# Loads of x and of the rearranged Wo: 32 partitions at a time, or all 128

## The chip, the cores and the metric

The kernel runs on one core of a Trainium2 chip. The time is that of the device, in microseconds, from one launch; the median of three runs is given, with the lowest and the highest. A profile of one further execution tells what each engine did: PE multiplies matrices (PEld loads its weights), DVE, ACT and POOL work elementwise, SP issues most of the transfers. Transfers (DMAs) run beside the engines, on 16 DMA engines that all queues share.

## The reference

One block of a transformer on x (2048 rows of 640, bf16): layer norm, then two branches that read the normed rows and are added to x.

```python
xn = _layernorm(x, axis=-1)
return x + _A_ref(xn, A_wqkv, A_wo) + _B_ref(xn, B_w_gate, B_w_up, B_w_down)

# A: 32 heads of 20, each row sees itself and the 255 rows before it (W = 256)
qkv = (x @ wqkv).reshape(B, S, 3, H, Dh)
scores = einsum("bhqd,bhkd->bhqk", q, k) * Dh ** -0.5
p = softmax(where(mask, scores, -1e9))
out = einsum("bhqk,bhkd->bhqd", p, v).reshape(B, S, D) @ wo      # wo: 640 x 640

# B: a gated MLP, F = 1536
h = sigmoid(x @ w_gate) * (x @ w_up)
out = h @ w_down
```

## The kernel before, in words

The 2048 rows are worked in four chunks of 512 rows (CW). A tile has 128 partitions (P); a chunk of x is a tile xc of 128 partitions by 4 blocks (SBC) of 640 columns, 1280 bytes a block. There is one such buffer (pool xp), so a chunk's load waits until the chunk before it is used up.

**x.** Chunk 0 is loaded 128 rows at a time (load_rows, L135). Chunks 1 to 3 are loaded by load_x (L113 to L118) in another order of rows: the chunk's row 128a + 32n + t lies in partition 32a + t, block n. This order lets the later transposition of 32 by 32 blocks (turn_block, L244) and a pass through memory (turn_rows, L249 and L251) give the normed rows transposed, as xnT, which every product with weights reads. load_x makes one transfer for each a: it fills the partitions 32a to 32a + 31, all four blocks. load_x(1) stands at L700, load_x(2) within qk1 (behind its first block of k, L723), load_x(3) after the norms of chunk 2 (L724).

**Normalization.** ln_block (L208, L214 on DVE) takes mean and variance of one block of columns of xc, rstd_blocks (L222, L223 on POOL) the factor of all four, norm_block (L227) applies them.

**q and k.** proj_block (L266) makes 128 columns of q or k transposed in PSUM. DVE (q) or ACT (k) copies them to a tile st (L270, L272; six buffers), which frees the PSUM bank, and SP stores st to a scratch in memory (sq, sk, L274). spread (L287) loads the scratch back in the layout of the scores, as qT and kT. The scratch holds 32 rows for each head of 20; POOL clears the other 12 once (clear, L156). So that these clears do not compete with x, POOL first copies two numbers of chunk 1 of x to a tile, landed (L703), which waits for that chunk to land.

**Scores and values.** PE makes scores ps (L500), ACT their exponentials pT (L506), POOL and DVE mask them (select at L489, masks at L517), PE multiplies by v (acc, L533), DVE divides and transposes (L544 to L567) to oc.

**MLP and output.** g_gu: products pg and pu (L414, L423), tanh on ACT (L417), h on DVE (L427). g_out: y gathers h times w_down (L437) and oc times wo (L444); DVE adds x's rows (L448), which SP loads (L454) ahead of time and stores as output (L459).

**wo.** The rows of Wo must be in the order of oc. POOL copies Wo in memory to wo_i (turn_wo, L179), eight transfers handed out one by one in qk1, each behind a projection block. wo_i is laid out by group i (4), then 160 rows. load_wo (L182 to L185) later fills the tile wo with four transfers, each 32 partitions by 5 blocks of 640.

**Order of work.** All is written in one order. PE's work is mixed by a planner (class Fill): attention steps come in their order, and between them parts of the rest (fill.add, L726 to L745) are drawn by estimated cost. PSUM tiles of all but the scores come from one ring of four banks (ps_d): a product waits until the bank four tiles back has been read. Each engine and each queue works in order. SP's transfers go round eight semaphores, and a transfer waits until the one eight before it has landed.

The functions that the change touches:

Of the kernel before, what the change touches and what calls it, by code (L numbers as in the profile page):

```python
# [9 lines left out]
P = 128  # L10
S = 2048
D = 640
H = 32
DH = 20
F = 1536
DC = D // P
FC = F // P
CW = 512
NCH = S // CW
SBC = CW // P  # L20
HG = 4
NG = H // HG
# [13 lines left out]
BF16 = mybir.dt.bfloat16  # L36
# [33 lines left out]
def kernel(  # L70
# [11 lines left out]
    nc = tc.nc  # L82
    x2 = A_x.flatten_outer_dims()
# [27 lines left out]
    xc = {}  # L111

    def load_x(c):  # L113
        t = xp.tile([P, SBC, D], BF16, name="xc")
        xc[c] = t
        rows = x2[c * CW:(c + 1) * CW, :].rearrange("(a n t) d -> a t n d", a=SBC, n=SBC)
        for a in range(SBC):
            nc.sync.dma_start(out=t[32 * a:32 * a + 32], in_=rows[a])  # L118

    wqkv = const.tile([P, DC, 3 * D], BF16, name="wqkv")  # L120
    wqkv_r = A_wqkv.rearrange("(c p) n -> p c n", p=P)
# [3 lines left out]
    wo = const.tile([P, DC, D], BF16, name="wo")  # L125
# [28 lines left out]
    def clear(w):  # L154
        rows = scratch[w].rearrange("(h j) s -> h (j s)", j=32)[:, DH * CW:]
        nc.gpsimd.dma_start(out=rows.rearrange("h (a e) -> h a e", a=4), in_=zero[:, 0:3, :])  # L156
# [14 lines left out]
        for lo, hi in ((0, 3), (3, 6), (6, 8), (8, 10), (10, FC)):  # L171
            nc.sync.dma_start(out=wd[:, lo:hi, :], in_=wd_r[:, lo:hi, :])

    wo_i = tc.dram_tile([HG, NG * DH, D], BF16, name="wo_i")

    def turn_wo(r, side):
        to = wo_i.rearrange("i (r a d) n -> r a i (d n)", a=2, d=DH)
        rows = A_wo.rearrange("(a r i d) n -> r a i (d n)", a=2, i=HG, d=DH)
        nc.gpsimd.dma_start(out=to[r, side].rearrange("i (e w) -> e i w", e=16),  # L179
                            in_=rows[r, side].rearrange("i (e w) -> e i w", e=16))  # L180

    def load_wo():  # L182
        for i in range(HG):
            nc.sync.dma_start(out=wo[32 * i:32 * i + 32, :, :],
                              in_=wo_i[i].rearrange("(m j) n -> j m n", j=32))  # L185


    ident = const.tile([P, P], BF16, name="ident")
# [263 lines left out]
    def new_rows(c, s, name="rows", bufs=3, queue=nc.sync):  # L452
        rows = lnp.tile([P, D], BF16, name=name, bufs=bufs)
        queue.dma_start(out=rows, in_=xr[:, c * SBC + s, :])  # L454
        return rows
# [242 lines left out]
    banks.close()  # L698
    ps_s = banks.enter_context(tc.tile_pool(name="ps_s", bufs=1, space=bass.MemoryType.PSUM))
    load_x(1)  # L700
    load_gu(wg, B_w_gate, 0, FS // 2)
    landed = const.tile([P, 2], BF16, name="landed")
    nc.gpsimd.tensor_copy(out=landed, in_=xc[1][:, 0, 0:2])  # L703
    clear("q")
    clear("k")
    for k, _ in enumerate(g_qk(0)):
# [11 lines left out]
    def later(load, *args):  # L718
        load(*args)
        yield 0  # L720

    behind1 = {("qk"[n // 4], 1 + n % 4): (lambda n=n: turn_wo(n // 2, n % 2)) for n in range(2 * NP)}
    behind1["k", 0] = lambda: load_x(2)  # L723
    norms2 = itertools.chain(g_norms(2, True), later(load_x, 3))  # L724
    norms3 = g_norms(3, False)
    fill.add("gu0a", mix(g_gu(0, 0, 6), g_first(rstds1), 0), 6 * GU)  # L726
# [3 lines left out]
    fill.add("v1", mix(g_v(1), norms2, 2, 1, False), 40 * 136)  # L730
    fill.add("rest1", later(spread_rest, 1), 0)
    fill.add("wo", later(load_wo), 0)
    fill.add("gu0c", mix(g_gu(0, 9, 12), norms2, 0, 1, False), 3 * GU)
    fill.add("gu1a", mix(g_gu(1, 0, 2), norms2, 0, 1, False), 2 * GU)
# [46 lines left out]
    c = NCH - 1  # L781
# [5 lines left out]
    rows = [new_rows(c, s, queue=nc.scalar) for s in range(SBC - 1)]  # L787
# [58 lines left out]
```

## Time and profile before

| | |
|---|---|
| median of 3 runs | 308.87 us (308.83 to 309.37) |
| the profiled execution | 309.65 us, its span 308.0 us |
| PE busy | 302.9 us |
| ACT / DVE / POOL busy | 193.2 / 184.4 / 83.8 us |
| granted clock of PE | 1.00 |
| moved by DMA | 36.86 MB, 120 GB/s over the span |

Times in the profile are counted from the first instruction. A line of the timeline gives the start, the length, the engine, the source line, the operation, what it writes and reads, how often, and in brackets how long the engine stood before it and what ended that wait. SPq is SP's queue of issues: its lines tell when a transfer was issued, not when it landed. A row of the stages gives the busy times of the engines in a stretch, the granted clock, the mean busy share of the 16 DMA engines (it can pass 1, since packets overlap) and what they moved.

### The profile page before, as it was taken

Reading aid. Unit: us, or ns where it says so; the run is one execution under the profiler, and the core shown is the slowest. Engines: PE = TensorE matmul, PEld = TensorE weight load, DVE = VectorE, ACT = ScalarE, POOL = GpSimd, SP = SyncE. Lnnn points to the kernel's source line nnn. Section 1 sums busy time; section 2 is a strip of 40 time slices with the busy share of each in tenths; the row PEclk is TensorE's granted clock in tenths of the full one; section 3 lists DMA queues with packets and bytes.
Section 4 is the critical chain, followed back from the end, with each engine's and each line's share of the span. In section 5 each row is a group of like instructions: output and inputs, shape, how many; then the busy total and the mean of one; then the engine's idle time right before and its main releaser. Section 6 shows DMA issues by size and latency. Waiting matters only on the chain.

```text
span 308.0 us, 10147 instructions
## 1 busy us (share of the span) xinstructions
PE 302.9 (98%) x4431; PEld 168.2 (55%) x4431; DVE 184.4 (60%) x378; ACT 193.2 (63%) x183; POOL 83.8 (27%) x189
## 2 busy tenths in 40 slices
PE   7999999999999999999999999999999999999996
PEld 3654445564456655654456655644546765444774
DVE  5787449298984579577642666454383627465523
ACT  6923785977766458867655557777766466778000
POOL 5011234635314133422213122241314132221100
PEclk9999999999999999999999999999999999999999
DMA  7997739889927222721152113550000210000301
GB/s 213 347 306 238 266 102 309 220 248 320 198 94 199 85 72 93 228 80 47 43 128 72 39 65 99 163 192 2 3 2 2 70 41 23 2 2 2 88 21 64
DMA packets 35756, 36.86 MB, mean 120 GB/s; under 512 B 2944, under 2 KB 35456, under 8 KB 35712
## 3 DMA queue, kind: packets, MB, share of 16 engines
q1 hardware_dynamic: 34304, 33.84, 36.6%
q0 software_dynamic: 544, 1.61, 1.7%
q10 hardware_dynamic: 864, 0.77, 0.9%
q8 instruction: 34, 0.56, 0.8%
q14 instruction: 10, 0.08, 0.1%
HBM read 25.59 MB, written 11.44 MB: 120 GB/s over the span
## 4 chain that ended last, share of the span: by engine, by line
PE 97%; DMA 1%; ACT 1%; DVE 0%; issue 0%; SPq 0%
PE pg L414 18%; PE y L437 18%; PE pu L423 17%; PE pqk L266 15%; PE ps L500 9%; PE y L444 7%; PE acc L533 6%; PE pv L324 6%; PE pv L304 1%; DMA xc<-in_A_x_dram 1%; PE pvh L304 0%; PE pt L233 0%; ACT turn L640 0%; ACT turn L645 0%; DVE turn L651 0%
## 5 line engine op out<-in xcount | busy, mean ns | idle before, releaser
L506 ACT ACTIVATE pT<-ps 128x2048 bf16<-128x2048 f32 x75 | 140.8, 1877 | 56.0 <-PE ps L500 33.4
L489 POOL TENSOR_SCALAR_AFFINE_SELECT pT<-pT 64x256 bf16<-64x256 bf16 (+1 forms) x126 | 67.5, 536 | 181.0 <-ACT pT L506 122.9
L414 PE MATMUL pg<-xnT,wg 128*128 128x512 bf16 x240 | 59.9, 380 | 0.0
L423 PE MATMUL pu<-xnT,wu 128*128 128x512 bf16 x240 | 59.8, 380 | 0.0
L427 DVE SCALAR_TENSOR_TENSOR h<-th,pu 128x512 bf16<-128x512 f32 x48 | 32.9, 685 | 42.8 <-ACT th L417 25.7
L437 PE MATMUL y<-wd,h 128*128 128x320 bf16 (+2 forms) x396 | 56.8, 295 | 0.0
L266 PE MATMUL pqk<-xnT,wqkv 128*128 128x512 bf16 x200 | 45.8, 381 | 0.0
L437 PEld LDWEIGHTS <-h 128*128 128x128 bf16 x396 | 36.8, 98 | 15.9 <-issue 2.3
L517 DVE TENSOR_TENSOR pT<-pT,keep 128x512 bf16<-128x512 bf16 (+2 forms) x81 | 35.4, 444 | 15.6 <-ACT pT L506 14.7
L417 ACT ACTIVATE th<-pg 128x512 f32<-128x512 f32 x48 | 28.6, 595 | 20.2 <-PE pg L414 19.9
L423 PEld LDWEIGHTS <-wu 128*128 128x128 bf16 x240 | 22.3, 98 | 27.3 <-issue 2.2
L414 PEld LDWEIGHTS <-wg 128*128 128x128 bf16 x240 | 21.7, 98 | 26.4 <-issue 2.9
L266 PEld LDWEIGHTS <-wqkv 128*128 128x128 bf16 x200 | 22.6, 119 | 19.0 <-issue 1.5
L500 PE MATMUL ps<-qT,kT 20*64 20x320 bf16 (+4 forms) x1440 | 32.0, 260 | 0.0
L544 DVE STREAM_TRANSPOSE t<-acc 128x512 f32<-128x512 f32 x32 | 21.0, 694 | 17.9 <-PE acc L533 17.9
L448 DVE SCALAR_TENSOR_TENSOR rows<-y,rows 128x320 bf16<-128x320 f32 x30 | 14.4, 489 | 24.2 <-PE y L444 24.2
L500 PEld LDWEIGHTS <-kT 20*64 20x64 bf16 x1440 | 13.5, 103 | 27.2 <-issue 26.7
L444 PE MATMUL y<-wo,oc 128*128 128x320 bf16 (+2 forms) x165 | 24.2, 295 | 0.0
L533 PE MATMUL acc<-pT,v 64*32 64x320 bf16 (+4 forms) x1440 | 20.3, 253 | 0.5 <-issue 0.5
L533 PEld LDWEIGHTS <-v 64*32 64x32 bf16 x1440 | 17.0, 92 | 4.2 <-issue 1.6
L444 PEld LDWEIGHTS <-oc 128*128 128x128 bf16 x165 | 15.5, 98 | 6.7 <-issue 1.0
L324 PE MATMUL pv<-wqkv,xnT 128*64 128x320 bf16 x240 | 17.4, 300 | 0.0
(61 smaller groups left out, 173.3 us busy)
## 6 DMA issues: line engine op xcount, KB each, us to landing
qT<-sq SPq DMA_DIRECT2D x16, 256.0 KB, 4.2
kT<-sk SPq DMA_DIRECT2D x16, 256.0 KB, 4.3
xc<-in_A_x_dram SPq DMA_DIRECT2D x16, 160.0 KB, 4.0
sq<-st SPq DMA_DIRECT2D x20, 128.0 KB, 3.6
sk<-st SPq DMA_DIRECT2D x20, 128.0 KB, 2.9
out_dram<-rows SPq DMA_DIRECT2D x15, 160.0 KB, 1.8
wg<-in_B_w_gate_dram SPq DMA_DIRECT2D x4, 480.0 KB, 7.2
wu<-in_B_w_up_dram SPq DMA_DIRECT2D x4, 480.0 KB, 7.4
```

The costliest lines, as they stand in the source:

```text
L266: nc.tensor.matmul(ps, lhsT=wt[:, m, :], rhs=xnT[c][:, :, d, :], start=(d == 0), stop=(d == DC - 1))
L324: nc.tensor.matmul(ps[hf * U:(hf + 1) * U, 0:HALF], lhsT=xnT[c][:, s, d, rows], rhs=wqkv[:, d, 2 * D + hf * HALF:2 * D + (hf + 1) * HALF], ...
L414: nc.tensor.matmul(pg, lhsT=part(wg, d, f), rhs=xnT[c][:, :, d, :], start=(d == 0), stop=(d == DC - 1))
L423: nc.tensor.matmul(pu, lhsT=part(wu, d, f), rhs=xnT[c][:, :, d, :], start=(d == 0), stop=(d == DC - 1))
L427: nc.vector.scalar_tensor_tensor(out=h, in0=th, scalar=1.0, in1=pu, op0=ADD, op1=MULT)
L437: nc.tensor.matmul(y[:, 0:cut[1] - cut[0]], lhsT=ht[c, f][:, s * P:(s + 1) * P], rhs=wd[:, f, cut[0]:cut[1]], start=(f == 0), stop=False)
L444: nc.tensor.matmul(y[:, 0:cut[1] - cut[0]], lhsT=oc[c, m][:, s * P:(s + 1) * P], rhs=wo[:, m, cut[0]:cut[1]], start=False, stop=(m == DC - 1))
L489: nc.gpsimd.affine_select(out=part, in_=part, pattern=pattern, compare_op=GE, fill=0.0, base=-1 if sign > 0 else 0, channel_multiplier=sign)
L500: nc.tensor.matmul(ps[side * U:(side + 1) * U, i, col * U:(col + n) * U], lhsT=qk["k", kc, half][32 * i:32 * i + DH, 2 * r + side, kb * U: ...
L506: nc.scalar.activation(out=pt[:, :, 0:used, :], in_=ps[:, :, 0:used * U], func=EXP, scale=SCALE)
L517: nc.vector.tensor_tensor(out=part, in0=part, in1=limit.to_broadcast([P, HG, n * U]), op=MIN)
L533: nc.tensor.matmul(accs[side][32 * i:32 * i + 32, q * U:(q + n) * U], lhsT=vt[sb][rows, b, at:at + 32], rhs=pt[rows, i, col:col + n, :], s ...
```

## The change

Three places.

load_x makes its four transfers by block n instead of by a: each fills one block of 640 columns in all 128 partitions. Where each row lands is the same. The copy landed, which waits for the chunk, now reads the last block.

wo_i is laid out as the tile wo wants it: by m (5), then 128 rows i, j. load_wo makes two transfers, of 3 and 2 blocks over 128 partitions. turn_wo writes to that layout; pieces of 20 rows that cross a border of 32 are cut in two, which makes twelve transfers on POOL's queue instead of eight. Uncut pieces are described as 16 parts of 1600 bytes for each of the 4 groups, as before; cut ones as n parts of 1280 bytes, n being their rows (4, 8, 12 or 16).

The products, their operands, and the order of all engines' other work stay the same.

```diff
     def load_x(c):
         t = xp.tile([P, SBC, D], BF16, name="xc")
         xc[c] = t
-        rows = x2[c * CW:(c + 1) * CW, :].rearrange("(a n t) d -> a t n d", a=SBC, n=SBC)
-        for a in range(SBC):
-            nc.sync.dma_start(out=t[32 * a:32 * a + 32], in_=rows[a])
+        rows = x2[c * CW:(c + 1) * CW, :].rearrange("(a n t) d -> n a t d", a=SBC, n=SBC)
+        for n in range(SBC):
+            nc.sync.dma_start(out=t[:, n, :], in_=rows[n])
...
-    wo_i = tc.dram_tile([HG, NG * DH, D], BF16, name="wo_i")
+    wo_i = tc.dram_tile([D, D], BF16, name="wo_i")
 
     def turn_wo(r, side):
-        to = wo_i.rearrange("i (r a d) n -> r a i (d n)", a=2, d=DH)
-        rows = A_wo.rearrange("(a r i d) n -> r a i (d n)", a=2, i=HG, d=DH)
-        nc.gpsimd.dma_start(out=to[r, side].rearrange("i (e w) -> e i w", e=16),
-                            in_=rows[r, side].rearrange("i (e w) -> e i w", e=16))
+        to = wo_i.rearrange("(m i j) n -> m i (j n)", i=HG, j=32)
+        rows = A_wo.rearrange("(a r i d) n -> r a i (d n)", a=2, i=HG, d=DH)[r, side]
+        at, end = (2 * r + side) * DH, (2 * r + side + 1) * DH
+        first = at
+        while at < end:
+            m, j = divmod(at, 32)
+            n = min(end - at, 32 - j)
+            e = 16 if n == DH else n
+            nc.gpsimd.dma_start(
+                out=to[m][:, j * D:(j + n) * D].rearrange("i (e w) -> e i w", e=e),
+                in_=rows[:, (at - first) * D:(at - first + n) * D].rearrange("i (e w) -> e i w", e=e))
+            at += n
 
     def load_wo():
-        for i in range(HG):
-            nc.sync.dma_start(out=wo[32 * i:32 * i + 32, :, :],
-                              in_=wo_i[i].rearrange("(m j) n -> j m n", j=32))
+        rows = wo_i.rearrange("(m p) n -> p m n", p=P)
+        for lo, hi in ((0, 3), (3, DC)):
+            nc.sync.dma_start(out=wo[:, lo:hi, :], in_=rows[:, lo:hi, :])
...
-    nc.gpsimd.tensor_copy(out=landed, in_=xc[1][:, 0, 0:2])
+    nc.gpsimd.tensor_copy(out=landed, in_=xc[1][:, SBC - 1, 0:2])
```

## The prediction

> **What bounds the kernel now.** I read the table of busy times first, then the chain, then the DMA speeds by stage, and last the queues around the transfers that are changed.
>
> ```profile
> span 308.0 us, 10147 instructions
> PE 302.9 (98%) x4431; PEld 168.2 (55%) x4431; DVE 184.4 (60%) x378; ACT 193.2 (63%) x183; POOL 83.8 (27%) x189
> PE 97%; DMA 1%; ACT 1%; DVE 0%; issue 0%; SPq 0%
> ```
>
> PE is busy 302.9 of 308.0 us, the chain that ended last is 97% PE, and PE's order is fixed in the program. So no transfer made faster can give back more than the few gaps that PE has, and a transfer made slower costs time only where PE, or an engine that frees its PSUM banks, comes to wait for it. The question is the slack behind each changed transfer.
>
> The speed of the transfers, by stage (PE, PEld, DVE, ACT, POOL busy, clock, DMA share, GB/s):
>
> ```profile
> 8.00:10.00 2.00, 2.00 (x19) 1.35 (x17) 1.71 (x6) 1.92 (x6) 0.00 (x0) 1.00 1.06 395
> 15.00:17.00 2.00, 2.00 (x11) 1.07 (x10) 1.30 (x2) 0.11 (x1) 0.00 (x0) 1.00 1.12 213
> 79.00:83.00 4.00, 3.45 (x107) 1.83 (x105) 4.00 (x9) 3.68 (x3) 0.96 (x2) 1.00 1.09 193
> 146.00:147.00 1.00, 1.00 (x20) 0.45 (x20) 0.41 (x1) 0.91 (x2) 0.14 (x1) 1.00 1.01 361
> ```
>
> From 8 to 10 us the weights wqkv come in over 128 partitions: 395 GB/s over 16 engines at a share of 1.06 is 23.3 GB/s an engine, or 55 ns for a row of 1280 B; from 146 to 147 us (turn, 128 partitions) it is 57 ns. From 15 to 17 us it is chunk 1 of x, over 32 partitions at a time: 213/16/1.12 = 11.9 GB/s, 108 ns a row. From 79 to 83 us it is mostly wo, also over 32 partitions: 116 ns. So transfers over 32 partitions do run at half speed here, with all sixteen engines busy.
>
> Who is behind chunk 1 of x on SP's queue, and how near:
>
> ```profile
> 10.28 1.76 SPq L118 DMA_DIRECT2D xc<-in_A_x_dram  x4
> 12.09 0.43 SPq L159 DMA_DIRECT2D wg<-in_B_w_gate_dram  x1
> ...
> 26.69 0.37 SPq L287 DMA_DIRECT2D kT<-sk  x1
> 27.12 0.46 SPq L159 DMA_DIRECT2D wu<-in_B_w_up_dram  x1
> ```
> ```profile
> 21.69 1.76 ACT L272 CAST st<-pqk 128x512 bf16<-128x512 f32 x3 [1.48 <-DMA sq<-st]
> ```
> ```profile
> POOL landed L703 <- DMA xc<-in_A_x_dram: 14.5, 1, 14.5
> ```
> ```profile
> 23.75 1.24 PE L414 MATMUL pg<-xnT,wg 128*128 128x512 bf16 x5
> ...
> 31.75 0.60 PE L423 MATMUL pu<-xnT,wu 128*128 128x512 bf16 x2
> ```
>
> POOL stands 14.5 us for x (free: it only gates the clearing of the scratch). But ACT has already waited 1.48 us, until 21.69, for the first store of q (sq<-st, issued at 14.95 behind x and wg) to land, because the seventh st tile reuses the first of six. That copy frees the PSUM bank of PE's pg at 23.75: it ends at 21.69 + 0.59 = 22.28, a slack of 1.47 us. And the second half of wu, issued at 27.12, lands 4.06 us later (31.18) and is read by pu at 31.75: 0.57 us of slack. These two are what the change can break.
>
> **The change, part by part.**
>
> *x, chunk 1.* Removed: four transfers, each filling 32 partitions with four rows each. Added: four transfers of the same 160 KB and 128 rows, each filling one of the four column blocks of all 128 partitions. SP issues four either way (1.76 us, unchanged; transfers whose two sides differ in shape, sq<-st, take 0.52 us an issue and not 0.43, which with nothing due on SP until 14.95 costs nothing). What is new is the source's shape: its outermost count is now 4 (blocks of 32 rows, 81,920 elements apart), and inside them 32 rows 640 apart. These strides can't be merged into one count of 128. Every transfer of the kernel before has at least 16 in the outermost place on both sides (128, 32, or 16 in wo_i), so no row of this trace shows how one with 4 is dealt out. The bounds: all sixteen engines, 8 rows each; or one engine per block, four engines with 32 rows each. I take four, since dealing out the outermost count is the only even cut that both sides offer without merging.
>
> Then one engine moves 128 rows for the chunk. Row time: 55 to 57 ns by the rows over 128 partitions, 108 ns by the row of x itself; the destination now spans 128 partitions and only four engines write, so I take 58 ns: 128 × 0.058 = 7.4 us. Now it takes 2.9 us (wu before it was issued at 6.52 and lands 9.8 later, at 16.3; POOL is released by the last x at 19.2). The last x lands 4.5 us later, and what stands behind it on those four engines moves by as much.
>
> [...]
>
> What follows, in order: sq's first store lands 4.5 later, so ACT's copy moves from 21.69 to 26.2; the bank is free at 26.8, and PE's pg stands from 23.75 to 26.8: 3.0 us. ACT makes its four copies by 26.2 + 4 × 0.59 = 28.5 (24.5 before), so the last store of k is issued 3.9 later, and with it kT<-sk (26.69 → 30.6; before, it waited for that store to land). The clearing of the scratch, which kT also waits for, starts 4.5 later than at 19.74 and took about 4.5 us, thus about 29.6 at the latest: not last. wu comes after kT on SP, 3.9 later, lands at 35.1 and is needed at 31.75 + 3.0 = 34.75. PE's total loss here is 3.9 − 0.57 = 3.3 us. The two waits overlap; the larger counts.
>
> Also behind: DVE's statistics. Each block now needs its own transfer alone, so only the last waits (ends 1.03 us after it, 24.7, against 23.3). POOL works out the scale after two clears, norms start some 3 us later, turn and xnT of chunk 1 shift by 2.5 to 3.5, and qk1 at 45.48, which reads xnT, shifts by 3.3. xnT's last transfer lands at 40.27 + 2.9 = 43.1: 2.3 us of slack. Nothing more.
>
> *x, chunk 2* (issued at 56.47): 7.4 us in place of about 2.3 (the landings run from 60.0 to 62.3). Behind it stand the stores of k and qT, kT of chunk 1, landing up to 5 us later. kT's landed at 68.9 and its first use is the scores at 78.04: 9 us of slack. wd's first part is needed at 82.79 and landed at 74.5. Cost 0.
>
> *x, chunk 3* (94.97): about 5 us later as well; behind it stands the load of output rows 2, issued at 97.34, landed at 101.4, read by DVE at 102.69. It would land at 106; DVE stands some 3 us, PE does not, since the banks of these rows are next wanted at 108.44. Rows 3, waiting on an output store, land at about 107.7 against 107.44. Cost 0, with 1.5 us in hand.
>
> *wo.* Two transfers in place of four, over 128 partitions: 40 rows an engine at 57 ns, 2.3 us, in place of 40 × 0.116 = 4.6. They were issued from 74.6, landed by 86.1 and are first needed at 89.13; nobody waited, so this gain is worth 0.
>
> *wo_i.* Twelve transfers in place of eight on POOL: 4 × 0.516 = 2.1 us, one more after each of four pairs of selects. POOL was idle 1.70, 0.68, 1.22 and 1.31 us before the selects that follow; each 0.52 fits, the second with 0.16 to spare. Cost 0; without that cover 0.5 us for one set of masks. wo waits for all twelve, at 74.6; the last of eight landed at 64.7.
>
> **The sum.** Chunk 1 gives +3.3, all else 0. The profiled execution took 309.65 us (span 308.0 and 1.65 around it); it becomes 313.0. It stands 0.8 above the median of the runs, 308.87; that becomes 312.2.
>
> **The rivals.**
>
> *Not slower: all sixteen engines carry the new x* (or eight do). Then chunk 1 takes 32 × 0.055 = 1.8 us instead of 2.9, wo gains as above, and nothing that PE waits for moves: 308.9. For it: the halved speed over 32 partitions is real. Against it: the source's count of 4. PE's loss is the delay of x less 1.1 us (0.6 regained on ACT's copies, 0.57 of wu's slack), so it decides at 4.0 us for the chunk: four engines would need 31 ns a row; eight at 58 ns would do.
>
> *The four engines hinder each other.* [...] At 108 ns a row the chunk takes 13.8 us, 10.9 more: 9.8 lost there; chunk 3's rows land at 112, and with 0.9 of adding PE stands from 108.44 to 113: 4.7; chunk 2 gives 1 to 2. That is 325; halfway (82 ns) it is 6.5 + 1.6, 317. For it: 108 and 116 ns where sixteen engines share 32 partitions. Against it: here four write, and in step only by chance. [...]
>
> *POOL's four added transfers run into the masks* (the 0.16 above): 0.3 to 0.5 us, on top of either case.
>
> **How the numbers follow.** Four engines at 47 to 65 ns (310.9 to 313.2): 0.55. Four that hinder each other (314 to 325): 0.25. Sixteen or eight: 0.15. Something else: 0.05. I predict 312.2, the likeliest, whose own range is 310.5 to 314. The range for eight in ten runs from 308.7, sixteen engines, to 319, past the halfway case of the second rival. A change of 0.2% (0.6 us) is about what this kernel's measurement can tell; slower by more 0.82, within 0.13, faster 0.05: the removed time lies where PE doesn't wait, and faster needs a gap of PE that I have not found to depend on a transfer.
>
> **What would show it.** Right: the DMA share falls to about a quarter around 17 to 21 us, POOL's copy of landed runs at 23 to 24 instead of 19.2, ACT's seventh copy at about 26 with the wait put down to sq<-st, and a gap of PE ahead of pg (L422) that adds with one ahead of pu (L431) to about 3.3 us; wo faster, and no gap at 89 or 108. Wrong: landed at or before 19.2 and no gap; or landed after 27 and a second gap at 108; or gaps that come from POOL's masks.

## The result, and the profile after

The changed kernel takes 311.57 us (311.39 to 312.38, 5 runs) against 308.87: 2.7 us slower, a ratio of 1.009 (95% interval 1.0076 to 1.0103). Its profiled execution took 312.38 us with a span of 310.3, 2.3 more than the span before. The other 0.4 us lie outside the span: 312.38 − 310.3 = 2.08, where it was 309.65 − 308.0 = 1.65. The page's summary and its chain:

```profile
span 310.3 us, 10146 instructions
PE 303.3 (98%) x4431; PEld 168.5 (54%) x4431; DVE 184.8 (60%) x378; ACT 193.0 (62%) x183; POOL 86.2 (28%) x193
PE 92%; DMA 6%; SPq 1%; ACT 1%; DVE 1%; issue 0%; ACTq 0%
```

PE does the same work; 6% of the chain that ended last now runs through transfers. Apart from 5.19 us of wqkv's load at the start, the chain in order of time shows which: the store of q, and later the stores of k and wu's second half.

```profile
20.43 5.85 DMA sq<-st
...
28.10 2.13 DMA sk<-st
...
30.70 4.05 DMA wu<-in_B_w_up_dram
```

The stage in which x alone is loading (columns as in the stages before: busy times, clock, DMA share, GB/s):

```profile
16.00:17.00 1.00, 1.00 (x6) 0.53 (x5) 0.61 (x1) 0.00 (x0) 0.00 (x0) 1.00 0.27 99
```

A share of 0.27 of sixteen engines is about four engines; 99 GB/s over that share is 22.9 GB/s an engine, 56 ns for a row of 1280 B. Before, the stage from 15 to 17 us had a share of 1.12 and 108 ns a row. Where x is alone, each row is twice as fast, and a quarter of the engines moves them. The trace's single packets say the same: each row of x is one packet of 1280 bytes, and from 15 to 21 us three to five of them run at any time, mostly four.

When SP issued x, q's first store, kT and wu's second half:

```profile
10.89 4.42 SPq L118 DMA_DIRECT2D xc<-in_A_x_dram  x4
...
16.58 3.75 SPq L282 DMA_DIRECT2D sq<-st  x3
...
30.28 0.37 SPq L295 DMA_DIRECT2D kT<-sk  x1
30.70 0.46 SPq L159 DMA_DIRECT2D wu<-in_B_w_up_dram  x1
```

What follows from it on POOL, ACT and PE, by their timelines:

```profile
23.76 0.18 POOL L711 COPY landed<-xc 128x2 bf16<-128x2 bf16 x1 [19.05 <-DMA xc<-in_A_x_dram]
```
```profile
25.37 2.05 ACT L280 CAST st<-pqk 128x512 bf16<-128x512 f32 x4 [4.54 <-DMA sq<-st]
```
```profile
26.00 1.24 PE L422 MATMUL pg<-xnT,wg 128*128 128x512 bf16 x5 [1.48 <-ACT st L280]
...
34.80 1.25 PE L431 MATMUL pu<-xnT,wu 128*128 128x512 bf16 x5 [0.73 <-DMA wu<-in_B_w_up_dram]
```

The last x lands at 23.7 instead of 19.2. ACT waits 4.54 us for q's first store, not 1.48. PE stands 1.48 us for the bank that this copy frees, and 0.73 us for wu: 2.2 us in all, and there is no other gap over 0.2 us after the start. Two smaller things differ between the two executions and nearly cancel. PE begins its first products of v at 7.42 us instead of 6.72; single executions of all the kernels here have 6.70 to 7.42. And the execution before had a gap of 0.55 us at 82.49, which later executions lack or have at 0.18, of kernels with the old load of Wo too. Neither is shown to belong to the change.

### The profile page after: what moved, and what is told of

It is laid out like the page before. It is cut to its first block, busy times and chain, and to the rows that moved or that the text cites. A ratio compares the mean times of both kernels' runs of the same rounds, so it can differ in the third digit from the quotient of the medians.

```text
span 310.3 us, 10146 instructions
## 1 busy us (share of the span) xinstructions
PE 303.3 (98%) x4431; PEld 168.5 (54%) x4431; DVE 184.8 (60%) x378; ACT 193.0 (62%) x183; POOL 86.2 (28%) x193
## 4 chain that ended last, share of the span: by engine, by line
PE 92%; DMA 6%; SPq 1%; ACT 1%; DVE 1%; issue 0%; ACTq 0%
PE y L445 17%; PE pu L431 16%; PE pg L422 16%; PE pqk L274 13%; PE ps L508 8%; PE y L452 7%; PE acc L541 6%; PE pv L332 5%; DMA sq<-st 2%; DMA wqkv<-in_A_wqkv_dram 2%; PE pv L312 1%; DMA wu<-in_B_w_up_dram 1%; DMA sk<-st 1%; PE pvh L312 0%; SPq L135 0%; ACT st L280 0%
## 5 line engine op out<-in xcount | busy, mean ns | idle before, releaser
L280 ACT CAST st<-pqk 128x512 bf16<-128x512 f32 x20 | 11.1, 597 | 11.4 <-PE pqk L274 6.9
```

## The experiments

The time of the kernel before, measured beside each, is given with each run; on these chips its runs spread from 308.8 to 311.1 us, so the profile's gaps tell the cases apart better than the medians. The kernels with 2 blocks have two runs each, the others four to twelve.

**Chunk 1 alone.** The kernel before, with only chunk 1 of x in the new form; A is 4 here.

```diff
-        rows = x2[c * CW:(c + 1) * CW, :].rearrange("(a n t) d -> a t n d", a=SBC, n=SBC)
-        for a in range(SBC):
-            nc.sync.dma_start(out=t[32 * a:32 * a + 32], in_=rows[a])
+        if c == 1:
+            rows = x2[c * CW:(c + 1) * CW, :].rearrange("(a n t) d -> n a t d", a=A, n=SBC)
+            for n in range(SBC):
+                nc.sync.dma_start(out=t[:, n, :], in_=rows[n])
+        else:
...
-    nc.gpsimd.tensor_copy(out=landed, in_=xc[1][:, 0, 0:2])
+    nc.gpsimd.tensor_copy(out=landed, in_=xc[1][:, SBC - 1, 0:2])
```

> Only chunk 1 of x is loaded in the new form (source of 4 blocks of 32 rows); chunks 2 and 3 and Wo stay as before. Theory (the whole loss comes from chunk 1, on four engines): 311.6 us as the whole change, within 0.4, with a gap of PE of about 1.5 us ahead of pg and one of about 0.7 ahead of pu. Rival (loads of chunks 2 and 3 or of Wo carry part of it): nearer 308.9 than 311.6.

311.47 us against 309.73, ratio 1.0058 (1.0035 to 1.0080). PE's timeline:

```profile
25.60 1.24 PE L419 MATMUL pg<-xnT,wg 128*128 128x512 bf16 x5 [1.53 <-ACT st L277]
...
34.28 1.25 PE L428 MATMUL pu<-xnT,wu 128*128 128x512 bf16 x5 [0.61 <-DMA wu<-in_B_w_up_dram]
```

Both gaps are here, about as large as in the whole change (1.53 + 0.61 against 1.48 + 0.73). Chunk 1 carries the loss that the traces show.

**The number of blocks in the source: 16, 8 and 2.** The same edit with A = 16, 8 and 2; the destination and the bytes of each transfer stay as they are.

> Chunk 1 alone, each transfer still one block of 640 columns in all 128 partitions, still from a source of two counts, but of 16 blocks of 8 rows; the rows thus come in another order, so the attention and the sums of this chunk are those of other rows. Theory (the outermost count of the source sets the number of engines): 16 engines at 55 ns a row, 1.8 us for the chunk, landed at 18.5 or earlier, no gap of PE, 308.9 us within 0.4. Rival (a transfer whose sides differ in shape is slow, whatever the count): 311.6 us and landed at 23 to 24, as in the whole change.

> As the run with 16 blocks, but 8 blocks of 16 rows (rows again in another order). Theory: 8 engines, 64 rows each, 3.5 to 3.8 us, landed near 20; that is 0.8 later than before, less than the 1.1 that the prediction gave as the point from which it costs: 308.9 to 309.2 us. Rival (slow whatever the count): 311.6.

> As the run with 16 blocks, but 2 blocks of 64 rows. Theory: 2 engines, 256 rows each at 55 ns, 14.1 us, landed near 31; the loss grows by the 7 us that this is later than with four engines: 318 to 319 us, nearly all of it in PE's gap ahead of pg. Rival (slow whatever the count): 311.6.

| blocks of the source | last x read by POOL | PE's gap ahead of pg | ahead of pu | time | ratio to before |
|---|---|---|---|---|---|
| 16 | 19.32 | none | none | 309.58 | 0.9992 (0.9967 to 1.0017) |
| 8 | 19.61 | none | none | 309.48 | 1.0006 (0.9983 to 1.0029) |
| 4 | 23.36 | 1.53 | 0.61 | 311.47 | 1.0058 (1.0035 to 1.0080) |
| 2 | 29.48 | 7.49 | none | 318.87 | 1.0297 (1.0238 to 1.0356) |

The stage of x with 2 blocks, and then with 16:

```profile
17.00:22.00 5.00, 5.00 (x25) 2.73 (x24) 2.76 (x6) 0.59 (x1) 0.00 (x0) 1.00 0.13 49
```
```profile
15.00:17.00 2.00, 2.00 (x11) 1.06 (x9) 1.23 (x3) 0.11 (x1) 0.00 (x0) 1.00 1.10 262
```

Two blocks give a share of 0.13, two engines of sixteen, at 24 GB/s each; sixteen give all of them. With eight blocks no stage has x alone, but its packets of 1280 bytes can be told apart in the trace: from 17.5 to 18.5 us these packets fill a share of 0.50, eight engines, at 55 ns a row. On SP's queue the source's outermost count set how many engines carried x here (shares of 0.13, 0.27 and 0.50 for 2, 4 and 8 blocks, all sixteen with 16), and the shape as such cost PE nothing (no gap with 16 or 8): the rival falls. The size of the gain was wrong, though: with 16 blocks POOL read x not at 18.5 but at 19.3, no sooner than before. In this stage, which is mostly x with some rows of wg, an engine moved 262/16/1.10 = 14.9 GB/s, not 23; the packets of x took 82 ns (median of the chunk), against 99 in the kernel before. So even all engines and all partitions together did not bring the speed of wqkv's load, 23.3 GB/s an engine, here.

With two blocks the gap of 7.49 us is not all. PE's clock was granted at half (the 0.50 below) for a while afterwards:

```profile
32.00:34.00 2.00, 2.00 (x6) 0.73 (x5) 0.80 (x2) 1.11 (x3) 0.77 (x1) 0.50 0.89 337
```

The first five products pg after the gap took 2.29 us instead of 1.24. The loss of 318.87 − 309.73 = 9.1 us is then the gap and some 1.6 us of slow clock; the expectation put nearly all of it in the gap, so that it hit the time is in part luck.

**Wo alone.** The change without load_x's part.

> Only Wo's part of the change (two loads over 128 partitions, twelve transfers on POOL's queue); x as before. Theory (nobody waits for wo, POOL's added issues fit its idle time): 308.9 us within 0.3, wo's transfers about half as long in the DMA engines. Rival (POOL's four added issues delay the masks): 309.2 to 309.5, with PE gaps between 50 and 70 us.

309.47 us against 309.24, ratio 1.0013 (0.9999 to 1.0027); PE has no gap over 0.2 us after the start. The stage in which wo is loaded:

```profile
79.00:81.00 2.00, 2.00 (x33) 0.80 (x30) 2.00 (x5) 1.94 (x2) 0.48 (x1) 1.00 1.01 347
```

347/16/1.01 = 21.5 GB/s an engine, 60 ns a row in place of 116: wo does come in at twice the speed, and nothing gets sooner by it. POOL's four added transfers cost PE nothing by the trace, and the span doesn't grow: its median is 307.4 us, against 307.5 before. But the time has a part outside the span, and that part is larger: 1.99 to 2.10 us in all twelve runs, against 1.65 to 1.77 in all 33 of the kernel before. So Wo's part costs about 0.3 us that no gap of an engine shows. The whole change has it too (1.99 to 2.08), the runs with new loads of x alone don't. What it stands for isn't shown; in two kernels below that contain Wo's part and move the copies of k it is 1.79 to 1.94.

**Chunks 2 and 3 alone.** Chunk 1 and Wo as before.

```diff
+        if c == 1:
+            rows = ...   # as before, by a
+        else:
+            rows = ...   # the new form, by n
```

> Only chunks 2 and 3 of x in the new form; chunk 1 and Wo as before. Theory: 308.9 us within 0.4; DVE waits about 3 us for output rows 2 behind chunk 3, PE doesn't. Rival (late rows hold PSUM banks): a gap of PE near 108 and 309.5 to 311.

309.49 us against 309.24, ratio 1.0017 (1.0001 to 1.0032). DVE waits for the output rows behind chunk 3, as expected:

```profile
105.26 0.89 DVE L453 SCALAR_TENSOR_TENSOR rows<-y,rows 128x320 bf16<-128x320 f32 x2 [3.33 <-DMA rows<-in_A_x_dram]
```

PE has no gap there. The interval begins at a hair over 1; the trace has nothing that would stand for it, and the part of the time outside the span is as before.

**Chunk 3 from two blocks.** The edit of chunk 1 with A = 2, for c == 3 instead. This puts a price on the slack that chunk 3 has.

> The kernel before, but chunk 3 of x loaded from 2 blocks of 64 rows (rows of this chunk in another order, so its attention and sums are those of other rows). Theory (chunk 3 has slack until PE wants the PSUM banks of output rows 2 and 3, so a load that is late enough costs): 2 engines at 55 ns a row are 14.1 us, output rows 2 land near 112 instead of 101, DVE is through near 113, and PE, which wants their bank at 108.4, stands 4 to 5 us: 313 to 314 us. Rival (chunk 3 has more slack than that): 308.9.

316.39 us against 309.46, ratio 1.0222 (1.0202 to 1.0243). PE's timeline, DVE's, and the stage at the end of PE's gap:

```profile
112.77 4.42 PE L271 MATMUL pqk<-xnT,wqkv 128*128 128x512 bf16 x10 [4.96 <-DVE rows L453]
```
```profile
112.22 0.89 DVE L453 SCALAR_TENSOR_TENSOR rows<-y,rows 128x320 bf16<-128x320 f32 x2 [10.09 <-DMA rows<-in_A_x_dram]
```
```profile
112.00:114.00 2.00, 1.23 (x4) 0.42 (x4) 1.22 (x3) 0.00 (x0) 0.00 (x0) 0.50 0.30 88
```

The wait is the one expected, at the place expected: late rows hold the PSUM banks that PE wants for q. The gap, 4.96 us, fits; the time is 2 us over the expectation, because here too PE ran at half clock afterwards (0.50 until 117.2 us; ten products took 4.42 us, where the kernel before has about 2.3).

**The copies of k moved away from the ring of st.** The whole change, with one line more:

```diff
-        st = stp.tile([P, CW], BF16, name="st")
+        st = wd[:, m, 0:CW] if (w, c) == ("k", 0) else stp.tile([P, CW], BF16, name="st")
```

> The whole change, but the five copies of k of chunk 0 go to the still unused tile wd instead of the ring of six st buffers, so that ACT's copy no longer waits for the first store of q. Theory (this wait holds the PSUM bank of pg, and wu behind kT on SP's queue is the second, overlapping wait): the gap of PE ahead of pg is gone, the one ahead of pu grows to 1 to 1.5 us, 309.9 to 310.4 us. Rival (PE's loss comes from elsewhere, such as the late statistics on DVE): 311.6.

```profile
32.05 0.42 PE L508 MATMUL ps<-qT,kT 20*64 20x320 bf16 x16 [0.20 <-DMA kT<-sk]
...
33.71 1.25 PE L431 MATMUL pu<-xnT,wu 128*128 128x512 bf16 x5 [1.23 <-DMA wu<-in_B_w_up_dram]
```

The gap ahead of pg is gone, and the one ahead of pu has grown to 1.23, with 0.20 ahead of the scores. That is the pattern of two overlapping waits: the ring of st was the first one's cause. The gaps fell from 2.2 to 1.4 us. The time was to be 309.9 to 310.4, and is not: the median is 311.10 us against 309.24 (1.0072, 1.0042 to 1.0102), and two of ten runs lay over 313. Three of the ten, 312.69 to 315.04 us, show a mean granted clock of 0.993 to 0.994; the median of the other seven is 310.97. So the gaps are explained here, and the time only in part.

**Chunk 1 of x on POOL's queue.** The whole change, with

```diff
+        queue = nc.gpsimd if c == 1 else nc.sync
...
-            nc.sync.dma_start(out=t[:, n, :], in_=rows[n])
+            queue.dma_start(out=t[:, n, :], in_=rows[n])
```

> The whole change, but chunk 1 of x is issued by POOL's queue instead of SP's. Theory (what costs is that the stores of q, the second half of wg and wu stand behind 128 rows of x on the same four engines of one queue): sq's stores no longer stand behind x, ACT's copy waits 2 us or less, the gap ahead of pg is gone; what is left is the clearing of the scratch, which still waits for x: 308.9 to 310.0 us. Rival (x's own landing, by the statistics, is what PE waits for): 311 us or more.

```profile
22.56 0.59 ACT L281 CAST st<-pqk 128x512 bf16<-128x512 f32 x1 [0.67 <-DMA sq<-st]
```

x is in at 20.97, q's store costs ACT 0.67 us, and PE has no gap between 7 us and the end. That fits the theory, but this run doesn't separate it from its rival: the queue is not the only thing that moved, since x also lands 2.8 us sooner here. On POOL's queue the four transfers did not share four engines. In the trace x's rows are 128 packets of 5120 bytes, and around 17.5 us sixteen or seventeen of them run at once. What separates the two is the run before this one: there x is read at 22.95, nearly as late as in the whole change, and the gap ahead of pg is gone. So x's own landing is not what PE waits for there. The time is 310.42 us against 309.24 (1.0040, 1.0016 to 1.0065), above the expected 308.9 to 310.0; 0.3 us of it is the larger part outside the span (2.02 to 2.08). In the profiled execution (span 308.7) PE's first products of v took 2.87 us instead of 1.60, before any of this; whether that happens in all executions of this kernel isn't known.

**wu moved ahead as well.** The kernel with k's copies in wd, and wu's second half issued right behind wg's, at the end of the first stage, instead of behind the first kT.

```diff
     load_gu(wg, B_w_gate, 0, FS // 2)
+    load_gu(wu, B_w_up, 0, FS // 2)
     landed = const.tile([P, 2], BF16, name="landed")
...
-                if r == 0:
-                    load_gu(wu, B_w_up, 0, FS // 2)
```

> The whole change, with the copies of k of chunk 0 in wd as in the run before, and the second half of wu issued right behind that of wg instead of behind the first kT. Theory (the two waits, sq's store and wu, are the whole loss): both gaps gone; what is left is kT itself, 0 to 0.5 us ahead of the first scores: 309 to 309.7 us. Rival (something else in the change costs): 310.5 or more.

311.99 us against 309.46 (1.0085, 1.0060 to 1.0111): a miss.

```profile
33.71 0.42 PE L506 MATMUL ps<-qT,kT 20*64 20x320 bf16 x16 [2.15 <-DMA kT<-sk]
```

Both gaps are gone, and a third is there, as large as the two: kT is issued at 31.00 and PE waits 2.15 us for it. wu now stands in front of the stores of q and k on the queue. Here the loss isn't two separate waits that can be cleared away one by one: of the two orders tried on SP's queue, each left PE waiting for what came last, 1.4 us in all with wu behind kT and 2.15 with wu in front.

**The whole change again**, beside the last.

> The whole change once more, on the chip of these runs, beside the last one: 311.4 us within 0.4, with the same two gaps of about 1.5 and 0.7 us.

311.03 us against 309.46, ratio 1.0055 (1.0038 to 1.0071).

```profile
24.56 1.24 PE L422 MATMUL pg<-xnT,wg 128*128 128x512 bf16 x5 [0.56 <-ACT st L280]
33.30 1.25 PE L431 MATMUL pu<-xnT,wu 128*128 128x512 bf16 x5 [0.68 <-DMA wu<-in_B_w_up_dram]
```

The gap ahead of pu repeats (0.73 in the first execution, 0.68 here, 0.61 with chunk 1 alone), the one ahead of pg does not (1.48, 0.56, 1.53). PE wanted the bank at about the same time in these three (24.52, 24.00 and 24.07); what moved is ACT's copy behind q's store (25.37, 23.92, 24.96), and with it x, which POOL read at 23.76, 22.33 and 23.36. So the gap ahead of pg was 1.48 and 0.56 in two executions of the same kernel. With it the loss is smaller here than in the first result: 1.6 us, of which 1.2 are in the spans (309.0 against 307.8), as much as the two gaps, and 0.3 outside them. No version that was run beats the kernel before.

## Why the prediction was right, point by point

The time, 312.2 forecast and 311.57 measured, and its cause were right: four engines, and then the two waits that were named. That the time came within 0.6 us is in part luck: the gaps were forecast at 3.3 us and were 2.2, and some 0.35 us outside the span were not in the sum. By its steps:

- *Four engines for a source of 4 blocks.* Right; shown by the share of 0.27 and by the runs with 16, 8, 4 and 2 blocks. Beforehand it was the author's estimate, taken from the shape of the source; no transfer of the kernel before showed it.
- *58 ns a row, 7.4 us for the chunk instead of 2.9, the last x 4.5 us later.* The delay was right, POOL reads x at 23.76, forecast 23.7; both lengths were too short by about as much, which is luck. By the packets of 1280 bytes the chunk ran from 14.09 to 23.14 us, 9.0 us, and before from 14.19 to 18.33, 4.1 us. A row took 55 to 56 ns where x was alone, but 91 (median) from 18.5 to 20 us, where other transfers ran beside it, and the four engines did not finish together. In the last run above, of the same kernel, the chunk took 7.6 us.
- *SP issues in 1.76 us as before.* Wrong, and not what the store waited for: the four issues took 4.42 us, 10.89 to 15.31, and q's first store was issued at 16.58 instead of 14.95. Its first packets (1024 bytes each) ran at 19.25 us all the same, 18.98 before; what was late is its share behind x. With 16 blocks the issues took 2.58.
- *q's first store 4.5 us later, PE's gap 3.0 us.* This is the term that was too large. The copy began 3.7 later (25.37 for 21.69), since less time passed between x and the store: 25.37 − 23.76 = 1.6 us, against 21.69 − 19.21 = 2.5 before. By their packets of 768 bytes, the rows of wg that stand between took 36 ns each on these four engines (median of the 160 of 640 that ran after 21.2 us), and 62 before (17 to 18.5 us). And in this execution PE wanted the bank at 24.52, not at 23.75. 3.0 − 0.8 − 0.8 leaves about the 1.48 that was measured.
- *wu 3.9 later, total 3.3.* kT was issued at 30.28, forecast 30.6; wu came at about 34.8, forecast 35.1; PE was 0.8 later by its start. 3.3 − 0.3 − 0.8 is the 2.2 of the two gaps.
- *Chunk 2, chunk 3, wo, wo_i: 0.* Right by the traces of the parts run alone, neither of which has a gap of PE. In the time it is not quite 0: the sum carries the 1.65 us around the span over unchanged, and with Wo's part it is about 2.0. For chunk 3 DVE waited 3.80 and 0.86 us, forecast 3 and 0.3, and the run with two blocks shows that the slack ends where the prediction put it. POOL's selects after the second group of transfers had no idle time left ahead of them, where 0.16 us was forecast.
- *Rival, sixteen or eight engines, no loss.* Did not happen, but was worked out rightly: both runs show no loss. The point from which it decides, between eight and four engines, holds. Its 1.8 us for the chunk does not: with 16 blocks x's packets ran from 13.97 to 18.41 us.
- *Rival, the four engines hinder each other.* Did not happen: four engines moved 99 GB/s and two moved 49, so an engine did about the same here with three others beside it (22.9 GB/s by the share) as with one (24). The slower rows from 18.5 to 20 us came while other transfers ran, not from the four alone.
- *Rival, POOL's added transfers run into the masks, 0.3 to 0.5 us.* Did not happen in Wo's run alone: PE has no gap there. The 0.3 us that Wo's part does cost lie outside the span, and that they are of the forecast size is chance.

## What to carry to other kernels

A transfer that filled all 128 partitions was not by that on all DMA engines here (a share of 0.27 with 4 blocks in the source, 0.13 with 2): look at the outermost count of the source, and at the DMA share while the transfer is alone. Here a transfer on four engines hurt less by its own lateness than by what was queued behind it on those engines (with x read as late as 22.95 us, but k's copies moved, the gap ahead of pg was gone), so price such a transfer at the waits of the next ones on the queue. Where an already hidden load gets faster, ask who was waiting for it; for wo nobody was. And compare the time outside the span as well as the span: a part of the loss was there (2.08 us against 1.65).

## What had not been expected of the hardware

All 128 partitions on all sixteen engines still did not give 55 ns a row for x: 14.9 GB/s an engine with 16 blocks of 8 rows, against 23.3 for wqkv, and 82 ns a packet of x (median of the chunk). With 8 and with 4 blocks a row took 55 to 56 ns where its packets were told apart or x was alone. What makes the rows slower with 16 no run shows.

While PE stood for 7.49 us (2 blocks, chunk 1) and 4.96 us (2 blocks, chunk 3), its clock was granted at half, from 4.0 and 2.5 us into the gap on, and it stayed there for 3.3 and 4.4 us after PE had gone on (to 35.0 and 117.2 us), 6.8 us in all both times. At half speed these stretches cost 1.6 and 2.2 us beside the wait itself. Gaps of 1.48 and 2.15 us had no such effect: the mean clock of those executions was 0.999, that of the two with the long gaps 0.989. So of these four gaps the two long ones cost more than their length and the two short ones did not; what sets the fall was not measured.
